# A decode kernel on one core: a new plan table, o turned in FP32, weight loads reshaped, fillers on three PSUM banks

## The chip, the cores and the metric

The kernel runs on one core of a Trainium2 chip. The metric is the device time of one execution in microseconds, the median of several runs. Single runs of one kernel differ by some per cent here: the kernel before took 310.5 to 320.4 us in the 44 runs of the four batches below, partly with the TensorE clock that the throttle granted (0.85 to 0.91; slower runs tend to have a lower one). A run more than 1.5% above the fastest of the same kernel counts as slow, and comparisons use the fast runs.

## The reference, cut to what matters

Four tokens (B=4), each with its own K/V cache, go through two identical layers. Both layers use the same weights and the same cache.

```python
def _A_ref(x, k_cache, v_cache, wq, wo):       # D=448, 16 query heads, 8 KV heads of Dh=256
    W = min(4096, max(256, Sk // 4))           # 2048 of 8192 cached positions
    q = (x @ wq).reshape(B, Sq, Hq, Dh) ...
    scores = einsum(q, k[last W]) * (Dh ** -0.5)
    o = einsum(softmax(scores), v[last W])
    return o.reshape(B, Sq, Hq * Dh) @ wo

def _B_ref(x, w_gate, w_up, w_down):           # F=1792
    return (silu(x @ w_gate) * (x @ w_up)) @ w_down

x = A_x
for _ in range(2):                             # written out twice in the reference
    x = x + _A_ref(_layernorm(x), ...)
    x = x + _B_ref(_layernorm(x), ...)
```

K and V of one head and one token are 1.05 MB each. Two layers would read every one of them twice, so the kernel keeps some heads in SBUF, the on-chip memory, from the first layer to the second. PSUM, named below, is the memory into which this kernel's matmuls write; the program calls its pieces banks.

## The kernel before: the parts concerned

A small scheduler takes all operations with modelled durations and fixes the order of each engine when the program is built. It places the semaphore waits, and it puts filler matmuls on zero weights into gaps of the tensor engine (PE), meant to keep its clock up (with more of them, in e6 below, the fast runs' clock is 0.90 to 0.91, against 0.87 to 0.90 in this kernel's of that batch). K and V go through 27 buffers of 512 KB. A table (`PLAN`, `OFF`, `KEEP_K`, `KEEP_V`) sets the order of heads and which of them are kept. K is scored against the query q; o is the attention's output before its projection by wo. It leaves PSUM with the wrong axis on the partitions, and the small matmuls that put that right are called the turn of o below.

```python
NPOOL = 27                       # K/V buffers
KEEP_K = (5, 5, 4, 5)            # heads kept between layers, by token
KEEP_V = (5, 5, 5, 3)
# ... (OFF and PLAN: the table)
TARGET = 3500                    # filler: PE columns wanted per WINDOW, a constant of the scheduler

# loads of weights: 448 rows are 3 x 128 and 64; the last 64 rows go in two column halves
# to partitions 0..63 and 64..127
for h in range(2):
    load(-80, 1 << 18, wq_sb[64 * h:64 * h + 64, 3 * 4096:], A_wq[384:448, 2048 * h:2048 * h + 2048], f"wq3{h}", 4096)
# ...
    for nm, wsb, src in (("wg", wg_sb, B_w_gate), ("wu", wu_sb, B_w_up)):
        load(rank, 3 * 458752, wsb[:, 0:3 * FF].rearrange("p (c n) -> p c n", c=3),
             src[0:384, :].rearrange("(c p) n -> p c n", p=128), nm + "a", 3584)
        for h in range(2):
            load(rank, 114688, wsb[64 * h:64 * h + 64, 3 * FF:], src[384:448, 896 * h:896 * h + 896], f"{nm}b{h}", 1792)

# end of a group of one or two heads: o from PSUM, split in a high and a low BF16 part, turned by PE
g.op(SCA, 0.34, pos, lambda e: e.activation(oh[:, :], Yb[p_][:, 256:512], ACT.Copy), ...)
g.op(DVE, 0.43, pos, lambda e: e.scalar_tensor_tensor(
    out=oh[:, :], in0=oh[:, :], scalar=lomask[:, 0:1], in1=Yb[p_][:, 256:512], op0=ALU.mult,
    op1=ALU.subtract), ...)
def flip(e):
    for dh in range(2):
        last = e.matmul(Yb[p_][:, 2 * n * dh:2 * n * dh + 2 * n],
                        lhsT=oh[:, :].rearrange("p (m e) -> p e m", e=2)[:, dh, :],
                        rhs=osel[:, 0:2 * n], start=dh == 0, stop=dh == 1, skip_group_check=True)
    return last
g.op(PE, 0.06, pos, flip, r=("oh", "osel"), ...)

# filler, into bank A only
g.filler = lambda e: e.matmul(
    Ab[:, 0:512], lhsT=zero[:, 0:1].broadcast_to([128, 128]),
    rhs=identb[:, :].unsqueeze(1).broadcast_to([128, 4, 128]), start=False, stop=False, skip_group_check=True)
```

## Time and profile before

| | before |
|---|---|
| time, median of the first three runs | 316.35 us (314.57 to 319.54) |
| profiled span | 309.4 us |
| read from memory in all | 108.31 MB |
| last cache byte, then until the end | 287 us, 22.4 us |
| query of the last token's second layer | 274.5 us |

The prediction shows the views of memory traffic. Three more views of the kernel before matter for what follows. First, busy time, share of the span and number of instructions of each engine:

```profile
PE 239.9 (78%) x4839; PEld 129.9 (42%) x4839; DVE 207.0 (67%) x645; ACT 70.9 (23%) x205; POOL 88.1 (28%) x233
```

Next the instructions at the end of an attention group, by line (engine, operation, tiles, shapes, count; busy us and mean ns; idle time before and its releaser):

```profile
L974 DVE SCALAR_TENSOR_TENSOR oh<-oh,small,Y 128x256 bf16<-128x256 bf16 x58 | 27.3, 471 | 12.2 <-ACT oh L972 11.8
...
L980 PE MATMUL Y<-tiny,oh 128*128 128x2 bf16 (+1 forms) x116 | 11.7, 170 | 5.8 <-DVE oh L974 5.0
...
L980 PEld LDWEIGHTS Y<-tiny,oh 128*128 128x128 bf16 x116 | 7.2, 100 | 16.0 <-DVE oh L974 11.9 <-issue 1.8 <-DVE small L948 0.9
```

and one turn of o on the timeline (start, length):

```profile
104.89 0.19 PE L980 MATMUL Y<-tiny,oh 128*128 128x2 bf16 x2
```

The turn of o is two matmuls in 0.19 us. Last, the DMA queue around the FFN's weights (start, us spent issuing, what): seven transfers go out within 9 us.

```profile
61.21 3.83 SPq L512 DMA_DIRECT2D wg_sb<-in_B_w_gate_dram  x3
65.09 3.72 SPq L512 DMA_DIRECT2D wu_sb<-in_B_w_up_dram  x3
68.85 0.59 SPq L512 DMA_DIRECT2D wd_sb<-in_B_w_down_dram  x1
```

### The profile page before, as it was taken

What the parts mean: (1) busy time and instruction counts of PE and PEld (TensorE: products, weight loads), DVE (VectorE), ACT (ScalarE), POOL (GpSimd) and SP (SyncE); (2) the same over time, 40 slices, a digit from 0 to 9 for tenths busy, and PEclk for the clock granted to TensorE, in tenths of its full rate; (3) what the DMA queues carried; (4) which work ended last, traced back from release to release, by engine and by line L of the source; (5) the groups of instructions that cost most, each with busy time, mean ns of one, the idle gap of its engine ahead of it and who ended that gap; (6) DMA issues with size and microseconds to landing.
All of it is one profiled execution on the core that took longest, in us unless ns stands there. A gap on an engine that the chain in (4) does not pass through costs nothing.

```text
span 309.4 us, 11130 instructions
## 1 busy us (share of the span) xinstructions
PE 239.9 (78%) x4839; PEld 129.9 (42%) x4839; DVE 207.0 (67%) x645; ACT 70.9 (23%) x205; POOL 88.1 (28%) x233
## 2 busy tenths in 40 slices
PE   4783867677688868886779888868878787987886
PEld 1321324234224534453355544424545543445563
DVE  8543377746254968989488888775798759775432
ACT  0030003121104313313231331222323312223410
POOL 1530103123104333333243432321333412335420
PEclk9579699999789978999795999999978999779965
DMA  6999999999999999999999999999999999989000
GB/s 267 343 383 399 391 400 405 392 394 337 313 394 397 401 392 402 386 357 383 373 364 379 397 400 401 392 395 341 397 399 398 394 397 397 387 307 332 9 3 3
DMA packets 43745, 108.31 MB, mean 350 GB/s; under 512 B 3240, under 2 KB 7344, under 8 KB 43312
## 3 DMA queue, kind: packets, MB, share of 16 engines
q1 hardware_dynamic: 43696, 107.60, 93.1%
q8 instruction: 38, 0.62, 0.8%
q14 instruction: 11, 0.09, 0.1%
HBM read 107.58 MB, written 0.00 MB: 348 GB/s over the span
## 4 chain that ended last, share of the span: by engine, by line
PE 39%; DMA 23%; SPq 16%; DVE 13%; issue 5%; ACT 2%; POOL 1%
DMA half<-in_A_v_cache_dram 13%; PE Y L957 8%; PE A L1081 7%; PE S L867 7%; DVE half L837 6%; SPq L512 6%; SPq L832 5%; SPq L845 5%; DMA wu_sb<-in_B_w_up_dram 5%; DMA half<-in_A_k_cache_dram 5%; PE Z L601 2%; PE A L1010 2%; DVE oh L974 2%; PE Y L927 2%; PE S L879 2%
## 5 line engine op out<-in xcount | busy, mean ns | idle before, releaser
L837 DVE STREAM_TRANSPOSE half<-half 128x1024 uint32<-128x1024 uint32 x90 | 110.5, 1233 | 11.3 <-DMA half<-in_A_k_cache_dram 11.1
L1081 PE MATMUL A<-identb,small 128*128 128x512 bf16 x211 | 74.6, 445 | 1.0 <-ACT wide L757 0.6
L970 POOL TENSOR_TENSOR small<-small 128x2 f32<-128x2 f32 (+1 forms) x58 | 42.5, 734 | 57.9 <-DVE small L948 57.3
L957 PE MATMUL Y<-half,pT 128*4 128x256 bf16 (+1 forms) x1024 | 46.4, 287 | 11.0 <-DMA half<-in_A_v_cache_dram 7.0
L867 PE MATMUL S<-half,qe 128*8 128x128 bf16 x1664 | 37.0, 232 | 11.3 <-DVE half L837 6.8
L884 POOL TENSOR_TENSOR qe<-qc,tiny 128x64 bf16<-128x64 bf16 x64 | 18.5, 294 | 84.0 <-PE S L867 62.6
L972 ACT ACTIVATE oh<-Y 128x256 bf16<-128x256 f32 x58 | 22.2, 383 | 79.4 <-PE Y L957 66.7
L974 DVE SCALAR_TENSOR_TENSOR oh<-oh,small,Y 128x256 bf16<-128x256 bf16 x58 | 27.3, 471 | 12.2 <-ACT oh L972 11.8
L867 PEld LDWEIGHTS S<-half,qe 128*8 128x8 bf16 x1664 | 26.5, 89 | 20.9 <-DVE half L837 9.6
L913 ACT ACTIVATE praw<-S,small 104x128 bf16<-104x128 f32 x52 | 19.1, 367 | 57.7 <-DVE small L905 55.1
L957 PEld LDWEIGHTS Y<-half,pT 128*4 128x4 bf16 (+1 forms) x1024 | 19.9, 85 | 22.8 <-DMA half<-in_A_v_cache_dram 11.5
L891 DVE TENSOR_REDUCE tiny<-S 104x1 bf16<-104x128 f32 (+1 forms) x58 | 17.3, 298 | 15.1 <-PE S L867 14.1
L1081 PEld LDWEIGHTS A<-identb,small 128*128 128x128 bf16 x211 | 20.2, 112 | 15.5 <-issue 8.2
L935 ACT ACTIVATE pT<-Y 128x64 bf16<-128x64 f32 (+1 forms) x58 | 13.6, 234 | 20.6 <-PE Y L927 17.8
L948 DVE TENSOR_REDUCE small<-Y 128x2 f32<-128x32 f32 (+1 forms) x58 | 10.6, 183 | 10.2 <-PE Y L943 10.0
L980 PE MATMUL Y<-tiny,oh 128*128 128x2 bf16 (+1 forms) x116 | 11.7, 170 | 5.8 <-DVE oh L974 5.0
L927 PE MATMUL Y<-sel,praw 104*128 104x32 bf16 x208 | 13.7, 180 | 3.0 <-ACT praw L913 2.9
L564 POOL TENSOR_SCALAR st<-st 128x1 f32<-128x1 f32 x16 | 4.3, 268 | 40.3 <-DVE st L553 40.3
L896 PE MATMUL S<-small,identb 104*104 104x32 bf16 x58 | 12.2, 219 | 4.1 <-DVE tiny L891 4.0
L1010 PE MATMUL A<-wo_sb,oT 128*4 128x448 bf16 x148 | 13.6, 376 | 1.9 <-DVE oT L990 1.8
L943 PE MATMUL Y<-pT,tiny 128*128 128x32 bf16 x64 | 11.1, 188 | 4.3 <-ACT pT L935 3.5
L927 PEld LDWEIGHTS Y<-sel,praw 104*128 104x128 bf16 x208 | 9.3, 98 | 11.8 <-ACT praw L913 6.8
(135 smaller groups left out, 276.1 us busy)
## 6 DMA issues: line engine op xcount, KB each, us to landing
half<-in_A_v_cache_dram SPq DMA_DIRECT2D x92, 512.0 KB, 10.3
half<-in_A_k_cache_dram SPq DMA_DIRECT2D x90, 512.0 KB, 10.4
wo_sb<-in_A_wo_dram SPq DMA_DIRECT2D x8, 448.0 KB, 13.5
wq_sb<-in_A_wq_dram SPq DMA_DIRECT2D x3, 1024.0 KB, 7.1
wd_sb<-in_B_w_down_dram SPq DMA_DIRECT2D x1, 1568.0 KB, 18.2
wg_sb<-in_B_w_gate_dram SPq DMA_DIRECT2D x1, 1344.0 KB, 15.5
wu_sb<-in_B_w_up_dram SPq DMA_DIRECT2D x1, 1344.0 KB, 17.1
wq_sb<-in_A_wq_dram SPq DMA_DIRECT2D x2, 256.0 KB, 11.2
```

The lines of the kernel that those rows point to most:

```text
L512: g.dma(rank, nbytes, lambda e: e.dma_start(dst, src), f"w{nw[0]}", w=key if isinstance(key, tuple) else (key,), run=run)
L837: return e.transpose(a, a)
L867: last = e.matmul(Sb[s_][qd:qd + 8, 0:128], lhsT=qe[q_][:, 0, ce, :, :].rearrange("p a n -> p (a n)"), rhs=kt[:, ce // 2, ce % 2, 2 * x:2 ...
L884: g.op(POOL, 0.25, pos - SLEAD - 1, lambda e, P=P, t=t, kvh=kvh: e.tensor_tensor(qe[q_][:, P, :, :, :], qc[t][:, kvh, :, :].unsqueeze(2).b ...
L913: return e.activation(praw[0:R, 2:258].rearrange("p (g r h l) -> p h g r l", g=2, h=2, l=2)[:, 0, :, :, :], Sb[s_][0:R, 0:128].rearrange(" ...
L927: last = e.matmul(o, lhsT=praw[0:R, c0:c0 + 128], rhs=w, start=(gg == 0 and h == 0), stop=False, skip_group_check=True)
L957: last = e.matmul(Yb[p_][32 * gg:32 * gg + M, 256:512], lhsT=pT[pt][:, gg, 2 * hv + a, 4 * P:4 * P + M] if n == 2 else p1[:, gg % 2, gg // ...
L970: g.op(POOL, 0.69, pos, lambda e: e.tensor_tensor(ri[p_][:, 0:2 * n], rs[p_][:, 0:2 * n], expo[:, 1:1 + 2 * n], op=ALU.pow), r=(f"rs{p_}", ...
L972: g.op(SCA, 0.34, pos, lambda e: e.activation(oh[:, :], Yb[p_][:, 256:512], ACT.Copy), r=(f"y{p_}",), w=("oh",), bank=(f"Y{p_}",))
L974: g.op(DVE, 0.43, pos, lambda e: e.scalar_tensor_tensor(out=oh[:, :], in0=oh[:, :], scalar=lomask[:, 0:1], in1=Yb[p_][:, 256:512], op0=ALU ...
L1010: last = e.matmul(Ab[32 * k:32 * k + B, 0:D], lhsT=oT[oi][:, k % 2, k // 2, :], rhs=wo_sb[:, 4 * kvh + k, :], start=False, stop=False, ski ...
L1081: g.filler = lambda e: e.matmul(Ab[:, 0:512], lhsT=zero[:, 0:1].broadcast_to([128, 128]), rhs=identb[:, :].unsqueeze(1).broadcast_to([128, ...
```

## The change

Its intent is to read less, to relieve VectorE, to load on all 128 partitions at once, and to hold the tensor engine at full clock. It has four parts. The table and its constants are new, with the K or V of 38 heads kept instead of 37 (the table is cut below to its head). ScalarE copies o out of PSUM in FP32, and FP32 matmuls turn it, so the subtraction on VectorE goes; pT, the transposed probabilities, is half as wide. The FFN's weights come in column halves, and each pair of 64-partition loads becomes one of 128 partitions. Fillers may go to three banks, with a higher target.

```diff
-KEEP_K = (5, 5, 4, 5)
-KEEP_V = (5, 5, 5, 3)
+KEEP_K = (6, 5, 5, 7)
+KEEP_V = (5, 5, 3, 2)
@@ (OFF, PLAN and eight lead and lag constants: new values; HOLD, HOLD_MIN, DMAX of the scheduler) @@
+FBANKS = ("A", "Z2", "Z")
-TARGET = 3500
+TARGET = 3600
@@ loads @@
-        for h in range(2):
-            load(-80, 1 << 18, wq_sb[64 * h:64 * h + 64, 3 * 4096:], A_wq[384:448, 2048 * h:2048 * h + 2048], f"wq3{h}", 4096)
+        load(-80, 1 << 19, wq_sb[:, 3 * 4096:],
+             A_wq[384:448, :].rearrange("r (h n) -> h r n", h=2), ("wq30", "wq31"), 4096)
@@ load_ffn @@
-                load(rank, 3 * 458752, wsb[:, 0:3 * FF].rearrange("p (c n) -> p c n", c=3),
-                     src[0:384, :].rearrange("(c p) n -> p c n", p=128), nm + "a", 3584)
                 for h in range(2):
-                    load(rank, 114688, wsb[64 * h:64 * h + 64, 3 * FF:], src[384:448, 896 * h:896 * h + 896], f"{nm}b{h}", 1792)
+                    load(rank, 3 * 229376, wsb[:, 0:3 * FF].rearrange("p (c n) -> p c n", c=3)[:, :, 896 * h:896 * h + 896],
+                         src[0:384, 896 * h:896 * h + 896].rearrange("(c p) n -> p c n", p=128), f"{nm}a{h}", 1792)
+                load(rank, 229376, wsb[:, 3 * FF:],
+                     src[384:448, :].rearrange("r (h n) -> h r n", h=2), (f"{nm}b0", f"{nm}b1"), 1792)
@@ o @@
-        oh = sb("oh", [128, DH], BF16)
+        oh = sb("oh", [128, DH], FP32)
-            g.op(DVE, 0.43, pos, lambda e: e.scalar_tensor_tensor(
-                out=oh[:, :], in0=oh[:, :], scalar=lomask[:, 0:1], in1=Yb[p_][:, 256:512], op0=ALU.mult,
-                op1=ALU.subtract), r=(f"y{p_}", "oh", "lomask"), w=("oh",), bank=(f"Y{p_}",))
-                                    rhs=osel[:, 0:2 * n], start=dh == 0, stop=dh == 1, skip_group_check=True)
+                                    rhs=rmask[:, 0:2 * n], start=dh == 0, stop=dh == 1, skip_group_check=True)
-            g.op(PE, 0.06, pos, flip, r=("oh", "osel"), w=(f"yp{p_}",), bank=(f"Y{p_}",))
+            g.op(PE, 0.25, pos, flip, r=("oh", "rmask"), w=(f"yp{p_}",), bank=(f"Y{p_}",))
@@ filler @@
-            Ab[:, 0:512], lhsT=zero[:, 0:1].broadcast_to([128, 128]),
+            fbank[b][:, 0:512], lhsT=zero[:, 0:1].broadcast_to([128, 128]),
```

## The prediction

> **What bounds the kernel now**
>
> I read the page first: span, and the row of GB/s in 40 slices. Then the same in stretches of my own, then the queue's waits, then the timeline of the end.
>
> ```profile
> span 309.4 us, 11130 instructions
> PEclk9579699999789978999795999999978999779965
> GB/s 267 343 383 399 391 400 405 392 394 337 313 394 397 401 392 402 386 357 383 373 364 379 397 400 401 392 395 341 397 399 398 394 397 397 387 307 332 9 3 3
> DMA packets 43745, 108.31 MB, mean 350 GB/s; under 512 B 3240, under 2 KB 7344, under 8 KB 43312
> ```
>
> For 37 of 40 slices the core reads memory at 390 to 400 GB/s. No engine is near that: DVE is busy 67%, PE 78% and a third of that is filler. So the first 287 us are transfer time, and what matters there is bytes, and the stretches that run below 395 GB/s. The last three slices move nothing. The next view (stretch, length, busy time of PE, PEld, DVE, ACT, POOL, then granted clock, DMA share, GB/s) cuts it finer.
>
> ```profile
> 10.00:14.00 4.00, 3.85 (x14) 1.71 (x14) 1.54 (x13) 0.00 (x0) 2.96 (x9) 0.50 1.01 276
> 73.00:84.00 11.00, 7.66 (x101) 3.20 (x99) 3.64 (x15) 1.17 (x3) 2.71 (x8) 0.84 1.06 293
> 272.00:279.00 7.00, 5.49 (x130) 3.34 (x122) 4.48 (x10) 1.63 (x3) 1.86 (x8) 0.76 0.78 288
> 279.00:287.00 8.00, 6.04 (x180) 4.60 (x183) 4.33 (x22) 2.90 (x9) 3.87 (x9) 1.00 0.88 305
> 287.00:296.30 9.30, 7.96 (x218) 5.06 (x206) 5.12 (x22) 3.49 (x10) 3.11 (x4) 0.97 0.02 4
> 296.30:309.40 13.10, 10.29 (x186) 6.91 (x186) 2.79 (x18) 0.55 (x2) 1.66 (x5) 0.50 0.01 3
> ```
>
> Two kinds of loss show. At 10 and at 73 us the DMA engines are busy (share above 1) and move too little: slow transfers. At 272 to 287 us the share itself drops: the queue has nothing it may issue. Then 22.4 us pass with no transfer: 9.3 us of attention that is behind its data, and 13.1 us of the last FFN at half the clock (0.50).
>
> ```profile
> SPq L793 <- DVE wo_sb L792: 27.8, 1, 27.8
> 275.13 1.77 PE L879 MATMUL S<-half,qe 128*8 128x256 bf16 x32 [1.05 <-POOL qe L884]
> 302.02 0.13 PEld L1081 LDWEIGHTS A<-identb,small 128*128 128x128 bf16 x2
> 302.05 1.44 PE L1081 MATMUL A<-identb,small 128*128 128x512 bf16 x3
> 303.28 1.68 PE L744 MATMUL Z<-wide,wd_sb 128*128 128x2 bf16 x56
> ```
>
> The queue's last cache load was issued 27.8 us before it could store the output. The query of the last token's second layer is only there at 274.5 us (the first scores after it start at 275.13), so its eight heads run from 274.5 to 293.6: 19.1 us. That chain, not the last byte, sets the end. The last three rows show fillers at half clock (three take 1.44 us) in front of a real matmul.
>
> [...]
>
> 1. [...] the two 64-partition pieces of wq are bytes 3.15 to 3.67 MB, and by single microseconds 11 to 13 us moved 205 and 229 GB/s against 400.
> 2. [...] the clock is 0.50 at 10 to 14 us and from 296.3 us on.
> 3. [...] the one FP32 matmul here (the norm's, 128x2) leaves two records, and costs 0.36 us against 0.20 us for the *two* BF16 matmuls of the turn of o.
> [...]
>
> **The change part by part**
>
> *New table and kept heads.* 38 heads' K or V are kept between layers instead of 37. The built programs have 82 K and 98 V halves instead of 90 and 92, so 180 instead of 182 of 0.524 MB: 1.05 MB less, at 396 GB/s 2.6 us. Eight transposes fewer: 8 x 1.233 = 9.9 us of DVE. Order matters more. Counting bytes along the queue, the last load of the last token's first layer stands at 93.4 of 107.6 MB before and at 90.8 of 106.5 MB after; it ended at 246 us before. And the last ten loads are all V, where the old table had K loads among the last.
>
> *One 128-partition load for two 64-partition ones* (wq, wg, wu). At 10 to 14 us the loss is 4 x (396-276)/396 = 1.2 us; at 73 to 84 us 11 x (396-293)/396 = 2.9 us, but that also holds the 896-byte rows of wd, which stay. I count 2.5 us of these 4.1 as regained. The column halves turn 3584-byte rows into 1792; V with 2048-byte rows runs at nearly the rate of K, so I count nothing.
>
> *o in FP32.* Removed: 58 DVE instructions of 0.471 us, 27.3 us of DVE and a hop per group between ACT (0.38) and the turn. Added: the turn goes from two BF16 (0.20) to two FP32 matmuls, 2 x 0.36 = 0.72 at most. Per group the chain loses 0.47 plus about 0.15 of hop and gains up to 0.52: within 0.1 us of nothing, better where the subtraction queued behind a 1.23 us transpose. PE gains at most 56 x 0.52 = 29 us of busy time in gaps that fillers would have taken. DVE in all loses 37 of 207 us: it is no bound, but transposes come sooner. The narrower pT, half the columns, saves ACT under 0.1 us a group.
>
> *Fillers on A, Z2, Z, target 3600.* 211 become 233. Worth: where the critical chain runs at half clock, chiefly the last 13.1 us. There I count delays behind fillers of 0.4 (norm), 0.25, 0.1, 0.4 (down projection), 0.6 (store) and 0.25 of slow matmuls: 2.0 us. I take half as likely regained, 1.0.
>
> *The sum* runs along two paths, and the later one decides.
> Transfers: 287 - 2.6 - 2.5 - 1.8 (half of the 3.7 us of gaps at 272 to 287) = 280. After the last V: 16 PV matmuls 0.6, ACT 0.4, turn 0.7, o 0.25, two column projections of 0.55, residual 0.2, hops 0.8: 4. Then 13.1 - 1.0: 296 to 297.
> Query: the last first-layer load lands at 246 - 2.63 MB/0.396 (6.6) - 2.5 = 237. The 28.5 us from there to the query (246 to 274.5) stay, less 1 for DVE's relief: 264.5. Eight heads 19.1, then 2.7 to the residual (293.6 to 296.3), then 12.1: 298.4.
> So about 298.5 of span against 309.4, 3.5% less. The timed runs (314.6 to 319.5) are longer than the profiled one (311.2); I scale, 316.35 x 298.5/309.4 = 305.2, and add a little for a plan that meets the chip less well than its author's model: 306.
>
> **The rivals**
>
> *The gain goes into new buffer waits.* Token 0 keeps 11 heads' halves, 22 of 27 buffers, where it kept 20. Only five stream while its first FFN runs. If the queue stalls there for 3 to 5 us, and later too, the time is 311 to 314. For it: the gaps at 272 us show such stalls exist. Against: at 60 to 92 us the old queue never starved (share 1.00 or more nearly throughout) and the FFN's weights fill that time.
> *FP32 turns take the PE's place as the bound.* If a turn costs 1 us or more, or leaves the clock low [...], each head's chain grows by 0.5 us; over the last eight, 3 to 4 us come back: about 310. Against: the norm's matmul at 0.36.
> *The clock is the whole story.* If half the runs' extra time over the profile (316 against 311) is low clock and the new fillers cure it, the timed runs come down to near the profile: 300 to 302.
> *Transfers hidden anyway.* If the query chain is not shortened because it waits for FFN and norm of an earlier token, only the last FFN gains: 312.
>
> **Range and chances**
>
> All main terms point down; the first and last rivals together get about a fifth. Predicted 306 us, range 299 to 313. Faster by over 2% means under 310.0: 0.77. Within 2%: 0.20. Slower: 0.03, as it would need a stall of over 15 us.
>
> **What would show it right or wrong**
>
> Right: no dip to 205-230 GB/s at 11 to 13 us and a shallower one at the FFN's weights; about 107.2 MB; the last cache byte at 278 to 283 us; first scores of the last token's second layer near 265; less than 20 us from last byte to end; the clock above 0.7 in the last 13 us; no DVE work between ACT's copy of o and its turn, the turn at 0.5 to 0.75 us. Wrong: a DMA share below 0.9 for 5 us or more after the first FFN; turns of 1 us; the last bytes after 285; a tail still at 0.50 (that alone costs 1 us).

Measured, for three statements that stand there without a number or with an estimate: in the kernel before, V's loads, with rows of 2048 bytes, land 10.3 us after their issue in the median, and K's 10.4; ScalarE's write of pT takes 224 ns in the median, and 198 in the changed kernel with the narrower pT; and the turn starts 0.06 us after the subtraction's end in one group (41.03 to 41.09 us) and 0.20 us after it in another (104.69 to 104.89).

## The result, and the profile after

The changed kernel is slower: 332.56 us median (330.47 to 334.75, four runs, all fast) against 315.46 us for the kernel before in the same rounds (312.99 to 319.54). The ratio is 1.057, with a 95% interval of 1.044 to 1.070. Here and below a ratio is the mean time of one kernel's fast runs over that of the other's fast runs of the same rounds, so it is not quite the ratio of the medians.

The page of the changed kernel gives span, busy times, clock and GB/s in 40 slices of 8.2 us each:

```profile
span 329.0 us, 11201 instructions
...
PE 277.3 (84%) x4921; PEld 160.5 (49%) x4921; DVE 177.2 (54%) x562; ACT 68.1 (21%) x199; POOL 87.5 (27%) x236
...
PEclk9999957999577989599799859956999995999965
...
GB/s 278 281 205 368 395 407 401 396 395 340 199 216 286 348 350 407 394 388 391 392 373 301 365 407 394 394 393 312 233 279 379 390 397 241 316 404 386 228 2 2
DMA packets 44934, 107.25 MB, mean 326 GB/s; under 512 B 3150, under 2 KB 8790, under 8 KB 44502
```

Bytes fell as predicted (107.25 MB). But the memory row, at 390 or more in 22 of 40 slices before, now has three kinds of holes: slices 2 and 3 (281 and 205), slices 11 to 15 (199, 216, 286, 348, 350), and later ones at slices 22, 28 to 30 and 34. PE is busy 84% instead of 78%, 277 us instead of 240. Single microseconds of the first two holes (stretch, length, busy time of PE, PEld, DVE, ACT and POOL, clock, DMA share, GB/s):

```profile
16.00:17.00 1.00, 0.75 (x9) 0.13 (x1) 0.15 (x1) 0.00 (x0) 0.62 (x2) 1.00 0.14 59
17.00:18.00 1.00, 0.00 (x0) 0.00 (x0) 0.00 (x0) 0.00 (x0) 0.00 (x0) 1.00 0.21 56
89.00:90.00 1.00, 0.81 (x20) 0.71 (x20) 0.30 (x2) 0.00 (x0) 0.27 (x1) 0.50 0.16 60
90.00:91.00 1.00, 1.00 (x14) 0.40 (x11) 0.50 (x5) 0.20 (x1) 0.81 (x2) 0.50 0.13 50
```

The rate falls to 50 to 60 GB/s, and the share of busy DMA time to 0.13. The share is a mean over 16 engines, and 2/16 is 0.125: from it the author estimates that about two engines were at work. No view shows single engines. The queue shows the same as time spent issuing. The five transfers after wq, whose last piece is a merged one, take 16.66 us, and the FFN's weights 6.13 + 8.52 + 4.78 = 19.4 us instead of 3.83 + 3.72 + 0.59 = 8.1 us:

```profile
1.15 2.00 SPq L513 DMA_DIRECT2D wq_sb<-in_A_wq_dram  x4
3.19 16.66 SPq L513 DMA_DIRECT2D wo_sb<-in_A_wo_dram  x5
...
72.09 6.13 SPq L513 DMA_DIRECT2D wg_sb<-in_B_w_gate_dram  x3
78.26 8.52 SPq L513 DMA_DIRECT2D wu_sb<-in_B_w_up_dram  x3
86.83 4.78 SPq L513 DMA_DIRECT2D wd_sb<-in_B_w_down_dram  x1
```

The end of an attention group has changed too. A turn now leaves four records, two for each FP32 matmul, by line:

```profile
L978 PE MATMUL Y<-small,oh 128*128 128x2 f32 (+1 forms) x224 | 37.5, 272 | 3.6 <-ACT oh L974 3.5
...
L978 PEld LDWEIGHTS Y<-small,oh 128*128 128x128 f32 x224 | 34.1, 214 | 11.8 <-ACT oh L974 7.4 <-issue 1.7 <-ACT wide L609 0.4
```

and on the timeline the four take 0.63 us, against 0.19 us:

```profile
113.75 0.63 PE L978 MATMUL Y<-small,oh 128*128 128x2 f32 x4 [0.25 <-ACT oh L974]
```

The chain that ended last, followed back from the end, has two larger entries: 10% of the span in the queue's issue of weight loads (L513; 6% at its counterpart before), and 8% in the turn itself (L978), which is not among the entries listed for before. PE's share of the chain is 52%, against 39% before:

```profile
PE 52%; SPq 16%; DMA 12%; DVE 11%; issue 4%; ACT 3%; POOL 2%; ACTq 0%
SPq L513 10%; PE Y L978 8%; PE Y L959 8%; PE A L1080 7%; PE S L869 7%; DVE half L839 6%; DMA wu_sb<-in_B_w_up_dram 5%; SPq L834 4%; DMA half<-in_A_k_cache_dram 4%; PE A L1008 3%; DMA half<-in_A_v_cache_dram 3%; PE Z L665 2%; PE S L881 2%; PE Y L929 2%; SPq L847 2%
```

The end of the kernel: a late hole at 235 us in which the queue waits for the tensor engine to free buffers (eight K loads take 17.8 us to issue from 227.1 us), then the last 19 us after the last byte, near 310 us. The clock in the final FFN is 0.56:

```profile
235.00:240.00 5.00, 4.42 (x129) 2.38 (x122) 3.80 (x8) 1.86 (x3) 1.41 (x6) 1.00 0.09 37
309.50:314.00 4.50, 4.01 (x86) 2.76 (x86) 2.00 (x14) 1.56 (x4) 1.97 (x5) 1.00 0.07 25
314.00:329.00 15.00, 12.71 (x233) 8.71 (x233) 3.32 (x22) 0.55 (x2) 2.46 (x8) 0.56 0.00 1
```

### The profile page after: what moved, and what is told of

Read it like the earlier page. It is cut to its first block, busy times and chain, and to the rows that moved or that the text cites. A ratio compares the mean times of both kernels' runs of the same rounds, so it can differ in the third digit from the quotient of the medians.

```text
span 329.0 us, 11201 instructions
## 1 busy us (share of the span) xinstructions
PE 277.3 (84%) x4921; PEld 160.5 (49%) x4921; DVE 177.2 (54%) x562; ACT 68.1 (21%) x199; POOL 87.5 (27%) x236
## 2 busy tenths in 40 slices
DMA packets 44934, 107.25 MB, mean 326 GB/s; under 512 B 3150, under 2 KB 8790, under 8 KB 44502
## 4 chain that ended last, share of the span: by engine, by line
PE 52%; SPq 16%; DMA 12%; DVE 11%; issue 4%; ACT 3%; POOL 2%; ACTq 0%
SPq L513 10%; PE Y L978 8%; PE Y L959 8%; PE A L1080 7%; PE S L869 7%; DVE half L839 6%; DMA wu_sb<-in_B_w_up_dram 5%; SPq L834 4%; DMA half<-in_A_k_cache_dram 4%; PE A L1008 3%; DMA half<-in_A_v_cache_dram 3%; PE Z L665 2%; PE S L881 2%; PE Y L929 2%; SPq L847 2%
## 5 line engine op out<-in xcount | busy, mean ns | idle before, releaser
L839 DVE STREAM_TRANSPOSE half<-half 128x1024 uint32<-128x1024 uint32 x82 | 100.5, 1233 | 9.2 <-DMA half<-in_A_k_cache_dram 8.7
L959 PE MATMUL Y<-half,pT 128*2 128x256 bf16 (+1 forms) x1024 | 47.8, 289 | 4.6 <-issue 2.2
L978 PE MATMUL Y<-small,oh 128*128 128x2 f32 (+1 forms) x224 | 37.5, 272 | 3.6 <-ACT oh L974 3.5
L978 PEld LDWEIGHTS Y<-small,oh 128*128 128x128 f32 x224 | 34.1, 214 | 11.8 <-ACT oh L974 7.4
L974 ACT ACTIVATE oh<-Y 128x256 f32<-128x256 f32 x56 | 21.5, 384 | 79.6 <-PE Y L959 70.7
L959 PEld LDWEIGHTS Y<-half,pT 128*2 128x2 bf16 (+1 forms) x1024 | 20.5, 84 | 17.9 <-issue 6.7
L988 DVE TENSOR_TENSOR oT<-Y,small 128x4 bf16<-128x4 f32 (+1 forms) x62 | 9.5, 161 | 32.2 <-PE Y L978 21.9
L937 ACT ACTIVATE pT<-Y 128x32 bf16<-128x32 f32 (+1 forms) x56 | 11.4, 204 | 31.1 <-PE Y L929 30.8
L950 DVE TENSOR_REDUCE small<-Y 128x2 f32<-128x32 f32 (+1 forms) x56 | 10.3, 184 | 10.6 <-PE Y L945 10.3
L929 PE MATMUL Y<-sel,praw 104*128 104x16 bf16 x192 | 12.4, 172 | 2.5 <-ACT praw L915 1.7
L907 DVE TENSOR_REDUCE small<-S 104x1 f32<-104x32 f32 x56 | 9.7, 179 | 8.0 <-PE S L901 7.7
```

What stands on the lines that cost most here:

```text
L839: return e.transpose(a, a)
L929: last = e.matmul(o, lhsT=praw[0:R, c0:c0 + 128], rhs=w, start=(gg == 0 and h == 0), stop=False, skip_group_check=True)
L959: last = e.matmul(Yb[p_][32 * gg:32 * gg + M, 256:512], lhsT=pT[pt][:, gg, 2 * hv + a, 2 * P:2 * P + M] if n == 2 else p1[:, gg % 2, gg // ...
L978: last = e.matmul(Yb[p_][:, 2 * n * dh:2 * n * dh + 2 * n], lhsT=oh[:, :].rearrange("p (m e) -> p e m", e=2)[:, dh, :], rhs=rmask[:, 0:2 * ...
```

## The experiments

All sixteen kernels gave results that passed against the reference. They ran in four batches of four, each batch on another chip. Before's medians were 316.4, 312.7, 314.4 and 316.0 us in these, so differences of 2 or 3 us between batches are not read. "Measured" gives the median of all runs, slow ones included; where kernels are compared, means of fast runs are used. A ratio's interval stands in brackets; of e1 and e8 the record has no ratio.

### Batch 1: the changed kernel and the old one, a part at a time

**e1, the changed kernel with its loads in pairs again**, each pair under one semaphore, so that the order of every engine stays the same.

```diff
-        load(-80, 1 << 19, wq_sb[:, 3 * 4096:],
-             A_wq[384:448, :].rearrange("r (h n) -> h r n", h=2), ("wq30", "wq31"), 4096)
+        load2(-80, 1 << 19, [wq_sb[64 * h:64 * h + 64, 3 * 4096:] for h in range(2)],
+              [A_wq[384:448, 2048 * h:2048 * h + 2048] for h in range(2)], ("wq30", "wq31"), 4096)
@@ wg and wu in the same way @@
```

> The changed kernel, every engine's order unchanged, but each of the three merged loads (wq, wg, wu remainders) issued again as two transfers of 64 partitions under one semaphore. Theory (the merged load[...] runs on two of the 16 DMA engines, share 0.13): the holes at 15-18, 88-92 and 98-100 us go, 12 to 15 us come back: 317 to 321 us, ratio to before 1.00 to 1.02. Rival (the new table holds too many buffers, or the FP32 turns slow each head): the holes at 177, 236 and 276 us stay and so does most of the time: 326 us or more.

Measured: 318.59 us median, two fast runs of 311.90 and 316.48 and two slow ones of 320.70 and 326.65. The dips at the weights are gone: slices 11 and 12 move 290 and 388 GB/s, where the changed kernel has 199 and 216. The fast runs average 314.2, so the merged loads cost the changed kernel about 18 us (14 by the medians, half of e1's runs being slow). Even so it is no faster than before, whose fast runs of this batch average 315.0. The later holes stay (168 in slice 29, 199 in slice 34), as the expectation's rival said, but the kernel is far from the rival's 326 us.

**e2, the kernel before with the merged loads alone.** The order of the compute engines is identical to before's.

```diff
-        for h in range(2):
-            load(-80, 1 << 18, wq_sb[64 * h:64 * h + 64, 3 * 4096:], A_wq[384:448, 2048 * h:2048 * h + 2048], f"wq3{h}", 4096)
+        load(-80, 1 << 19, wq_sb[:, 3 * 4096:],
+             A_wq[384:448, :].rearrange("r (h n) -> h r n", h=2), ("wq30", "wq31"), 4096)
@@ wg and wu in the same way @@
```

> The kernel before, every compute engine's order unchanged, with only the merged loads of the change. Theory (two DMA engines): 10 to 15 us slower than before, 326 to 331 us, with the DMA share at 0.13 after the first loads and in the FFN's weights. Rival [...]: 1 to 3 us faster, 313 us.

Measured: 328.54 us (327.29 to 333.54), ratio 1.043 [1.031, 1.054]. This one edit costs 13 us by fast runs. Its page shows the same two dips, in slices 3 and 4 and in 11 and 12, in an otherwise little changed row:

```profile
GB/s 281 319 178 291 398 400 403 397 390 325 200 223 355 365 371 398 400 356 357 392 369 371 398 400 399 393 400 367 375 399 395 399 394 399 394 320 306 8 3 2
```

and one microsecond in the second dip (columns as above) a share near 2/16 (0.14; in the first dip it falls only to 0.33):

```profile
88.00:89.00 1.00, 0.00 (x0) 0.00 (x0) 0.00 (x0) 0.00 (x0) 0.00 (x0) 0.81 0.14 54
```

The edit makes two loads of 64 partitions into one of 128, whose source's pattern `h r n` begins with h = 2. The author's theory, that such a load keeps two engines busy, is an estimate from the shares of 0.13 and 0.14; that the 2 in the pattern is the reason was not shown. The cost fits in size. The merged pieces are 0.52 + 0.23 + 0.23 = 0.98 MB, and at 57 GB/s (the mean of the changed kernel's windows of 16 to 18 us) an estimate is that they take 17 us; 13 us (here) to 18 us (e1) reach the end. That later transfers queue behind the merged ones, until the queue cannot issue, is the likely link; the issue times of the changed kernel agree (16.66 us), but no view here shows it.

**e3, the kernel before with the FP32 turn alone** (no subtraction on VectorE, pT half as wide), planned anew.

```diff
-        oh = sb("oh", [128, DH], BF16)
+        oh = sb("oh", [128, DH], FP32)
-            g.op(DVE, 0.43, pos, lambda e: e.scalar_tensor_tensor( ... op1=ALU.subtract), ...)
-            g.op(PE, 0.06, pos, flip, r=("oh", "osel"), ...)
+            g.op(PE, 0.25, pos, flip, r=("oh", "rmask"), ...)
@@ the mask in the turn, and the narrower pT: cut @@
```

> The kernel before with only the FP32 turn of o (schedule made anew with the change's own durations). If the turn costs what it did in the changed kernel (0.56 to 0.66 us against ACT-to-DVE-to-PE of 0.47 + 0.20 + a hop), it is within 1%: 313 to 319 us. Rival (the FP32 turns made the changed kernel slow): 320 us or more.

Measured: 340.04 us (333.86 to 341.49), ratio 1.069 [1.049, 1.088]. This part alone costs more than the whole change. PE is busy 85%, and the granted clock averages 0.76 to 0.80 over the four runs, where before has 0.86 to 0.89 in this batch.

**e4, the kernel before with the new table and constants alone.**

```diff
-KEEP_K = (5, 5, 4, 5)
+KEEP_K = (6, 5, 5, 7)
@@ and the rest of the table @@
```

> The kernel before with only the new plan table and its constants, kept heads included. As predicted (shorter query chain, 1 MB less): 308 to 313 us. Rival (22 of 27 buffers held starve the queue, holes near 177, 236 and 276 us): 320 us or more.

Measured: 312.78 us (309.51 to 319.22), ratio 0.985 [0.971, 0.999]. The table helps a little, by less than the bytes and the order suggested. Only two of its runs are fast, 309.5 and 310.4 us.

### Batch 2: the parts that help, and a rival for the turn

**e5, the kernel before with table, fillers and column halves**, o in two BF16 parts as before and the loads in pairs. Its diff is that of the change without the merged loads and without the section on o.

> The changed kernel without its two suspects: new table, fillers on three banks and column halves, but the BF16 turn of o and the 64-partition loads of before. Theory (the merged loads and the FP32 turn cost all that the rest gains): 305 to 311 us, 2 to 3% under before, clock 0.89 or more. Rival (some other part is bad too): 314 us or more.

Measured: 310.12 us (309.65 to 311.31), ratio 0.992 [0.988, 0.996]. Holes remain in its memory row, which the old table has not:

```profile
GB/s 271 332 391 399 392 409 400 394 396 353 292 383 395 359 408 395 390 385 394 392 404 370 406 398 390 397 392 352 175 382 395 388 398 219 377 336 351 195 2 4
```

The 175 in slice 29 and the 219 in slice 34 stand at the places of two of the changed kernel's late holes. So they don't need the FP32 turn. The table, which keeps more and leaves fewer buffers to stream through, is the likely cause of the second, which stays in e13 below (219). The first is not the table's alone: in e13, with the same table, slice 29 moves 333.

**e6, the kernel before with the fillers alone.**

```diff
+FBANKS = ("A", "Z2", "Z")
-TARGET = 3500
+TARGET = 3600
@@ and the scheduler's lines for three banks @@
```

> The kernel before with only the new fillers (banks A, Z2, Z, target 3600). As predicted, about 1 us gained: 312 to 316 us, clock a little above before's 0.86 to 0.89. Rival (more fillers get in the way of real matmuls): 318 us or more.

Measured: 310.03 us (307.36 to 312.27), ratio 0.988 [0.982, 0.995]. Table and fillers each bring some 1.2 to 1.5%, and together, with the column halves, 0.8%. They do not add, as far as differences of this size can be read.

**e7, e1 with the planner told the real length of the turn** (0.59 us instead of 0.135), so the order of all engines is planned for it. A rival cause is that only the plan was wrong about a harmless turn.

```diff
-            g.op(PE, 0.25, pos, flip, r=("oh", "rmask"), ...)
+            g.op(PE, 1.1, pos, flip, r=("oh", "rmask"), ...)     # the planner multiplies by 0.54
```

> The changed kernel with the loads in pairs, and the planner told 0.59 us for the FP32 turn in place of 0.135 us (it measured 0.56 to 0.66): the orders of all engines are made anew. Theory (the turn's cost is that the static order was planned for a turn of a quarter of its length): 4 to 9 us below the run with pairs, fast runs at 306 to 311 us. Rival (the PE's time itself is what costs, whatever the order): the same as with pairs, fast runs at 312 to 318 us.

Measured: 319.85 us (317.79 to 322.26), ratio 1.023 [1.015, 1.031]. That is no better than e1 (its fast runs average 314.2), so the rival falls.

**e8, e6 with the FP32 turn.** Here the new fillers, with which the clock was 0.90 to 0.91 in e6's fast runs, are there to hold it.

```diff
@@ e3's edit on top of e6's @@
```

> The kernel before with the FP32 turn and the new fillers. The run with the FP32 turn alone had a clock of 0.78 to 0.80 and took 334 to 341 us. If the clock is how the FP32 turn costs, the fillers bring it to 0.86 or more and the time to 318 to 326 us. Rival (the turn's own PE time in each head's chain): 332 us or more, whatever the clock.

Measured: 329.61 us, one fast run of 322.82 and three slow ones of 329.01 to 332.92, at a clock of 0.81 to 0.87. Against e6's fast runs (309.1 in the mean) the turn still costs 14 us, by the one fast run; by the medians, 20.

### Batch 3: what in the turn costs

All of these start from e8. e9, e10 and e11 keep its order on every engine, and e10 and e11 only add two matmuls to each turn.

**e9, o rounded once to BF16 and turned by two BF16 matmuls.** There is no low part, on purpose; the result passed, and how much less exact it is was not measured.

```diff
-        oh = sb("oh", [128, DH], FP32)
+        oh = sb("oh", [128, DH], BF16)
-                                    rhs=rmask[:, 0:2 * n], ...
+                                    rhs=rsel[:, 0:2 * n], ...
```

> The old plan with the new fillers, and o leaves PSUM once, in BF16, with no low part (the result is a little less exact, on purpose); the order of every engine is that of the run with the FP32 turn and new fillers (329.6 us), only the two matmuls of each turn are BF16 now. Theory A, the FP32 turn itself (its 0.6 us on the tensor engine for 58 groups) costs the 20 us: 308 to 312. Theory B, what costs is the rest of that edit (no subtraction on VectorE, so transposes and buffers come in another order): it stays at 322 to 330.

Measured: 307.83 us (306.87 to 309.54), ratio 0.983 [0.972, 0.994]. With the same order on all engines, the type of o and its mask is worth 15 us by fast runs (e8 has one), 22 by the medians. The rest of that edit costs nothing. The memory rows of e8 and e9 show where a part of the time goes:

```profile
GB/s 282 322 385 397 396 402 399 389 399 293 389 394 401 390 402 297 271 348 375 367 395 396 399 392 279 337 339 355 369 399 294 376 410 351 360 250 235 2 2 2
```

```profile
GB/s 271 334 383 400 390 401 407 393 393 355 337 393 372 396 397 399 382 366 337 382 389 393 395 398 401 393 398 388 395 395 382 390 397 399 379 350 334 15 2 3
```

The first row is e8's. It has holes (297 and 271 in slices 16 and 17, 279 in slice 25) which e9 with the same order has not. Its queue waits 175 us in all for the tensor engine to free K/V buffers, e9's 149 us. So here a tensor engine that is not the bound on average (busy 85% of the span in e8) still holds up the transfers.

**e10, e9 with two zero matmuls of 512 columns in each turn**, over the full array (128*128 in the trace), so that the turn takes at least as long as in FP32 (0.65 us, against 0.63).

```diff
+                if not isinstance(e, Tally):          # hidden from the planner: its order stays
+                    for _ in range(2):
+                        last = e.matmul(Yb[p_][0:128, 0:512], lhsT=zero[:, 0:1].broadcast_to([128, 128]),
+                                        rhs=identb[:, :].unsqueeze(1).broadcast_to([128, 4, 128]), start=False, ...)
```

> The same as the BF16 kernel of this batch, and two zero matmuls of 512 columns over the full array at the end of each turn (0.45 us or so), so that a turn takes the tensor engine about as long as with FP32, in work that keeps the clock up. If the time on the engine is what costs: 320 to 328. If FP32 costs because it leaves the clock low: 308 to 315.

Measured: 316.05 us (311.37 to 324.08, 21 runs), ratio 1.006 [1.002, 1.010], clock 0.91 to 0.96. By fast runs (313.9 in the mean) that is 6 us above e9 and 9 us below e8's one fast run, although its turns are no shorter.

**e11, the same with 32 columns of weights** instead of 128 in the two zero matmuls.

```diff
-                        last = e.matmul(Yb[p_][0:128, 0:512], lhsT=zero[:, 0:1].broadcast_to([128, 128]),
+                        last = e.matmul(Yb[p_][0:32, 0:512], lhsT=zero[:, 0:1].broadcast_to([128, 32]),
```

> As the run before it, but the two zero matmuls have 32 columns of weights instead of 128, so they take the same time and use a quarter of the array. If time alone counts, the same as with 128 (within 2 us). If what counts is whether the work holds the clock up, slower than with 128 by 5 us or more and with a lower granted clock, near 325 to 330.

Measured: 318.18 us (316.22 to 324.17), ratio 1.014 [0.996, 1.031], clock 0.93 to 0.96. The fast runs (316.2 and 316.9) lie 3 us above e10's mean, within the interval: the width of the weights (128*32 in the trace, and 0.59 us for the two matmuls as with 128*128) makes no clear difference, either to the time or to the clock. The second half of that expectation fell.

**e12, e9 planned anew with 0.06 us for the turn.**

```diff
-            g.op(PE, 0.25, pos, flip, ...)
+            g.op(PE, 0.06, pos, flip, ...)
```

> The old plan, new fillers, single BF16 copy of o, and the planner told 0.06 us for the turn as in the kernel before, so the order is planned for it. It drops 27 us of VectorE's subtractions at no cost on the tensor engine, on top of the fillers alone (310.0 us): theory that the path through VectorE matters: 303 to 308; rival, transfers set the pace: 309 to 312.

Measured: 306.38 us (305.56 to 306.77), ratio 0.978 [0.969, 0.987].

### Batch 4: the changed kernel's own plan, and the last question on the turn

**e13, e1 with e9's edit**: table, column halves and fillers of the change, loads in pairs, o once in BF16, the order of e1.

```diff
@@ e9's edit on top of e1 @@
```

> The changed kernel with the loads as pairs again (318.6 us with FP32), and o in BF16 once, its turn BF16; same order on every engine. If the FP32 turn is the second cause in the new plan too, 304 to 310. If the new table's own queue holes are what is left, 312 to 318.

Measured: 305.24 us (304.15 to 306.15), ratio 0.973 [0.963, 0.983].

**e14, e13 planned anew with 0.06 us for the turn** (e12's edit).

```diff
-            g.op(PE, 0.25, pos, flip, ...)
+            g.op(PE, 0.06, pos, flip, ...)
```

> The same with the planner told 0.06 us for the turn, so planned anew. If the table suits only the durations it was searched with, slower than the one before by some us; if not, within 2 us of it. Against the best so far (old table, 306.4 us): if the new table is worth what it saves in bytes, 303 to 305; if its holes cost as much, 306 to 310.

Measured: 305.27 us (302.66 to 309.54), ratio 0.970 [0.956, 0.985]. e13 and e14 beat both kernels, and differ from e12 by 1 us in the medians, which can't be read between batches. Once the rest is right, no gain of the new table is shown.

**e15, e9 with each turn done eight times**: 16 BF16 matmuls of two or four columns.

```diff
-                for dh in range(2):
+                for rep in range(1 if isinstance(e, Tally) else 8):
+                    for dh in range(2):
```

> The kernel with old table, new fillers and BF16 o (307.8 us), each turn done 8 times over, so 16 BF16 matmuls of 4 columns (0.5 to 0.7 us) instead of 2. If few-column work that mostly loads weights leaves the clock low, as the FP32 turn does: 320 to 330 at a clock of 0.88 or less. If only the time on the engine counts, as with the two wide zero matmuls: 312 to 318 at 0.92 or more. If low clock is special to FP32: the latter as well.

Measured: 333.45 us (329.65 to 335.65), ratio 1.053 [1.033, 1.073], clock 0.81 to 0.85. There is no FP32 in the turn, and the loss is e8's and more. It also adds 812 matmuls to the instruction stream. The chain that ended last has 5% of issue in it as in e9, so the chain does not put the time there.

The turns of e15 and e10 on the timeline, for comparison with the 0.63 us in FP32:

```profile
105.46 0.58 PE L978 MATMUL Y<-tiny,oh 128*128 128x2 bf16 x16
```

```profile
104.55 0.20 PE L977 MATMUL Y<-tiny,oh 128*128 128x2 bf16 x2
104.61 0.59 PE L982 MATMUL Y<-identb,small 128*128 128x512 bf16 x2
```

And the busy times and granted clock of the four kernels with one order, e9, e8, e10 and e15:

```profile
PE 251.0 (82%) x4859; PEld 133.1 (43%) x4859; DVE 184.3 (60%) x576; ACT 69.2 (22%) x205; POOL 88.2 (29%) x233
...
PEclk9999799879869955979995997998976999999965
```

```profile
PE 279.4 (85%) x4975; PEld 163.8 (50%) x4975; DVE 185.5 (57%) x576; ACT 69.4 (21%) x205; POOL 88.2 (27%) x233
...
PEclk9998799985999855799995687999858999999765
```

```profile
PE 263.4 (83%) x4975; PEld 136.4 (43%) x4975; DVE 184.5 (58%) x576; ACT 69.1 (22%) x205; POOL 88.1 (28%) x233
...
PEclk9998979999999959999997799997958999999985
```

```profile
PE 281.8 (86%) x5671; PEld 159.1 (48%) x5671; DVE 185.2 (56%) x576; ACT 69.5 (21%) x205; POOL 88.4 (27%) x233
...
PEclk9978989985998555799965855999957999998855
```

| kernel | turn, us | PE busy, us | span of the same execution | clock of all runs | fast runs, us |
|---|---|---|---|---|---|
| e9, two BF16 matmuls | 0.20 | 251 | 307.6 | 0.88 to 0.92 | 306.9 to 309.5 |
| e10, and 2 x 512 columns | 0.65 | 263 | 319.3 (slow) | 0.91 to 0.96 | 311.4 to 316.0 |
| e8, FP32 | 0.63 | 279 | 327.2 (slow) | 0.81 to 0.87 | 322.8 |
| e15, 16 BF16 matmuls | 0.58 | 282 | 329.5 | 0.81 to 0.85 | 329.7, 331.3 |

(0.65 is from the start of the first to the end of the last of e10's two rows, 104.55 to 105.20.) Time follows PE's busy time: 12, 28 and 31 us more of it than in e9 go with 12, 20 and 22 us more of span in the same executions. (The profiled executions of e8 and e10 are slow ones; the fast runs give the same order.) A turn that is longer by 0.4 us comes 58 times. In e8 and e15 it is spent loading weights for two or four columns (the turns' weight loads are busy 36.3 and 28.0 us, their matmuls 41.1 and 32.8 us), and the granted clock is low (0.81 to 0.87). In e10 it is spent streaming columns (weight loads 14.1 us, matmuls 48.1 us), the clock is higher (0.91 to 0.96, against 0.88 to 0.92 in e9), and other matmuls get shorter: a score matmul of the group of L868 takes 229 ns in the mean in e10, 238 in e9, 245 in e8 and 253 in e15. So a part of the loss is PE's time as such (e10, 6 us by fast runs), and the larger part goes with turns beside which the clock is low (e8 15 us, e15 22 us). FP32 is not needed for that: e15 loses it in BF16, and e15 against e10 shows, at nearly equal turn lengths, that the kind of work decides. That it does so through the clock, and not through e15's weight loads or its number of matmuls, fits all four runs but is argued. What sets the granted clock is not shown.

**e16, the changed kernel with e9's edit**, merged loads kept.

```diff
@@ e9's edit on top of the changed kernel @@
```

> The changed kernel (332.6 us) with its merged loads, only o and its turn in BF16; same order. If the two causes add: 332.6 less what BF16 saves in the run with paired loads (some 10 us), so 319 to 325. If the slow loads hide the turn's cost: 328 to 332.

Measured: 323.03 us (319.63 to 328.04), ratio 1.026 [1.010, 1.042]. With it the two causes make a table in the changed kernel's plan, all at one order of the engines (means of fast runs, us; e1 has only two, 311.9 and 316.5):

| | loads in pairs | merged loads | merging costs |
|---|---|---|---|
| o in BF16 | 305.2 (e13) | 321.9 (e16) | 16.7 |
| o in FP32 | 314.2 (e1) | 332.6 (the change) | 18.4 |
| FP32 costs | 9.0 | 10.7 | |

They add, within 2 us, which is less than e1's two fast runs differ. By the medians, in which slow runs of e1 count, FP32 would cost 13.4 and 9.6, and merging 17.8 and 14.0.

The best kernel of the study, e13, in the two rows that were read first of the kernel before:

```profile
span 304.1 us, 10980 instructions
...
GB/s 266 324 390 397 394 408 401 397 396 384 295 356 395 398 402 395 394 393 393 374 376 377 399 401 393 396 391 397 333 347 391 386 399 219 368 402 385 195 2 3
```

## Why the prediction was wrong

Predicted 306 us, range 299 to 313, with a chance of 0.03 for slower. Measured 332.6. Two terms of the sum failed. With the merged loads alone the kernel took 323.0 us (e16), with the FP32 turn alone 318.6 (e1, one of whose four runs, at 311.9, lies in the range).

**"One 128-partition load for two 64-partition ones" failed in its sign.** "I count 2.5 us of these 4.1 as regained": it lost 13 us (e2) to 18 us (the change against e1), by fast runs. The step put the slow pieces (205 and 229 GB/s against 400) down to their 64 partitions, and took one transfer over 128 to be served like the others. What limits the new transfer is not shown. Its source's pattern, as the diff shows, begins with a dimension of 2 (`h r n`); that this is the cause was not tested. The first check named for this step, no dip at the wq pieces, came out as a deeper dip: 57 GB/s instead of 205 and 229.

**"o in FP32 … within 0.1 us of nothing" failed in what it counted.** The length was right: 0.63 us, inside the predicted 0.5 to 0.75 and under the 0.72 at most. The subtraction on VectorE went, as said (VectorE's busy time fell by 30 us, not by 37). But it balanced the chain of one group and then put 29 us of PE's time "in gaps that fillers would have taken". Fillers did not give way: the changed kernel has 199 + 34 of them in its trace, the predicted 233, and 84 us of PE's time, where before has 211 and 75 us; e8 and e9 have the same 231. So the turn's time came on top: 28 us of PE's time in e8 against e9 made 20 us of span in the profiled executions and 15 us by fast runs, at a lower clock, and the queue waited 26 us more for buffers that PE had yet to free. The step rested on a misreading as well: "for 37 of 40 slices" at 390 to 400 GB/s. The row that it shows has 22 slices at 390 or more, so not all of the first 287 us were transfers at that rate, and e8 shows that PE's time was not free in them. The prediction's own rival for it asked for turns of 1 us before anything came back, and gave it 3 to 4 us. Its second half, a turn that "leaves the clock low", was the better reading (0.81 to 0.85 in e15 and 0.91 to 0.96 in e10 bear it out as far as they go), and the argument against it (the norm's single FP32 matmul at 0.36) spoke only of length.

**New table and kept heads: right in bytes, too hopeful in what follows.** 107.25 MB against "about 107.2". Alone it gives 1.5% (e4). The rival of new buffer waits was partly right: e5 shows holes with the new table and the old loads, and in the changed kernel 235 to 240 us moved 37 GB/s at a DMA share of 0.09, which the prediction had named as a sign of being wrong. They did not outweigh the table's gain (e4).

**Fillers: under-sized.** Counted at 1.0 us in the tail; alone they bring 1.2%, some 3.7 us (e6). The tail got less than was asked: the granted clock in the last 15 us is 0.56 in the changed kernel and in e6's last 13 us 0.68, where the prediction asked for over 0.7. Where the gain lies is not shown; most likely it is the mean clock, which is 0.90 to 0.91 in e6's fast runs and 0.87 to 0.90 in before's of that batch.

**The path.** The prediction said that the last token's query sets the end, at 264.5 us. It came at 292.1 in the changed kernel (274.5 before) and, with both causes removed, at 267.8 (e13). There the last bytes land near 285, and the end is 304.1 in the profile, 305.2 in the median. That e13 lands within 1 us of the predicted 306 is no merit of the prediction: e13 gains by o in a single BF16, which the change doesn't have, and loses by holes that the sum did not have.

From before to after, by fast runs, each against before in its own batch: table, fillers and column halves bring 0.8% (e5); dropping the subtraction with a single BF16 o makes it 2.7% (e13). The FP32 turn takes all of that away (e1, 314.2 against 315.0), and the merged loads make the kernel 5.7% slower.

What stays open: what sets the granted clock, how the FP32 turn's cost divides between PE's time and the clock, and whether a merged load whose source does not begin with a dimension of 2 would have brought the predicted gain. It needs another row order of the weights, which was not run.

## What to carry to other kernels

When two transfers are merged by rearranging one side, try the merged load alone before counting the gain, and look at the share of busy DMA time in the windows: here it fell to 0.13 at 50 GB/s (0.14 at 54 GB/s in e2), and the merged loads cost 13 us (e2). When work moves to an engine that is "78% busy, a third of it filler", price its time there and don't call it free (15 us lost for 28 us more of PE's time, e8 against e9), and ask whether it streams columns or mostly loads weights (with 0.59 us of wide matmuls in each turn the clock was 0.91 to 0.96, e10; with 0.58 us of 16 matmuls of two or four columns 0.81 to 0.85, e15). Change such parts one at a time: here the small gains of the table and the fillers hid which two parts did the harm, and how much.
